# Square roots of the key norms on ScalarE for the first two chunk pairs, with a new instruction order

## The chip, the cores and the metric

The kernel runs on one core of a Trainium2 chip. The metric is the device time of one launch in microseconds. The five engines are TensorE (PE; its weight loads are shown as PEld), VectorE (DVE), ScalarE (ACT), GpSimd (POOL) and SyncE (SP), which here issues every DMA. The instructions of each engine stand in the trace in the order of the program.

## The reference

A delta-rule attention, written as a loop over 768 steps for 4 batches and 8 heads of 48 features, and behind it a feed-forward network (FFN) on its output, with 3072 tokens, 384 features and 2048 hidden units:

```python
k_n = k / (np.linalg.norm(k, axis=-1, keepdims=True) + 1e-06)
for t in range(S):
    y[:, :, t] = np.einsum('bhd,bhde->bhe', q[:, :, t], state)
    v_old = np.einsum('bhde,bhd->bhe', state, kt)
    state = state + bt[:, :, :, None] * np.einsum('bhd,bhe->bhde', kt, vt - v_old)

h = x @ w_in                       # x: y, tokens by features
sp = np.maximum(h, 0.0) + np.log1p(np.exp(-np.abs(h)))
out = (h * erf(sp)) @ w_out
```

## The kernel before

The 768 steps are cut into 12 chunks of 64, two chunks making a pair. The loop inside a chunk becomes linear algebra: a Gram matrix of the keys (`gram_mm` with the name "pg"), scaled by `gn` = -beta / norm² (`gram_d` for chunks 0 and 1, `gram_a` for the others), then the inverse of a triangular matrix, then a short chain per batch (`chain_u`, `chain_s`, `chain_y`, 48 chain steps j in all) that carries the state from chunk to chunk. The inverse of pair 0 is worked out on VectorE (`first_blocks`, 15 times `first_row`, `first_back`) and finished on TensorE (`first_w`, `first_x`); that of every other pair by 31 `solve_row` on GpSimd, with a way through DRAM before and behind it. `merge_t` to `merge_m2` put the halves together. Four chain steps make an FFN group of 256 tokens, 12 groups g in all: `x_max` to `x_lo` scale and split the input into two halves of 16 bits, `ffn1` (16 blocks for each group, numbered n through all groups) makes h, `e_sp` (softplus), `e_erf`, `e_mul`, `e_split` and `e_rest` make the activation of a unit of two blocks, and `ffn2` multiplies by w_out. The weights come as 64-bit numbers, twelve blocks of 512 KB for each matrix, and are turned into two 16-bit halves on the way: `w_load`, `w_low` (a shift on VectorE), `w_mask` (ScalarE), `w_bits` (merges the two on VectorE), `w_sum`, then `w_hi` and `w_lo`.

**The key norms.** For each pair sg, `norm_sq` (L183) squares k on ScalarE and `norm_sum` (L191) sums over the 48 features on VectorE, chunk by chunk. Then `norm_ops(sg, 0)` to `norm_ops(sg, 5)` issue eighteen VectorE instructions on a 128x32 tile, three at a time (L202 to L215): the maximum with 1e-30, an integer first guess of the inverse root, three Newton rounds of three instructions, norm, + 1e-6, reciprocal, and from it gn and ga. norm itself (nm) scales v in `put_v`.

**Tables.** `table` (L125 to L128) loads a ScalarE table set when the set asked for isn't the one loaded last: set 2 for erf, Abs in `w_sum`, and `clear_first`; set 24 for softplus. The Prelu of `w_mask` isn't in set 24, so where it falls between two softplus calls the compiler adds two loads more (in the trace at 101.88 and 105.43 us).

**The order.** Every step is entered as an event with a due time (`on`), the events are sorted, and `ORDER`, a tuple of 2523 indices, then gives the order in which they are issued. It sets the order on all five engines and nothing else does. The events `fill` are products of zeros on TensorE: 150 of them, 128x384 in 16 bits, stand between real steps up to the first FFN block. Three PSUM banks are shared by the Gram and chain steps, and two banks by the `ffn1` results, each freed by an `e_sp` and an `h_out`.

**The beginning, in this order.** SyncE loads the transposed keys of chunk 1, k of chunks 1 and 0, the transposed keys of chunks 0 and 3, beta of pair 0, a block of v, then w_in blocks and q. ScalarE does the two Squares first. VectorE does the two sums, all six `norm_ops(0, i)`, seven `gram_d`, `first_blocks`, the rows with some weight steps between them, `first_back(0)` (L329, the other triangle's copy `xd`) and `first_back(1)` (L327, `td`). `first_w` on TensorE reads only `td`. `first_copy` on ScalarE and `first_x` read `xd`.

Of the kernel before, what the change touches and what calls it, by code (L numbers as in the profile page):

```python
# [11 lines left out]
AF = mybir.ActivationFunctionType  # L12
ALU = mybir.AluOpType
# [42 lines left out]
XR = 3  # L56
YR = 6
S2A = (0, 1, 2, 3)
CP = (0, 1, 2, 3)
CM = (0, 1, 2, 3)  # L60
FB = 6.5
T0 = 55.0
SW = 4.6
C1, C2 = 2.0, 14.0


EG = {("pg", 1, 1): 2, ("pq", 0, 0): 0, ("pq", 0, 1): 1}
SET_ERF, SET_SP = 2, 24
HSC = 2.0 ** -23


@with_exitstack
def delta_ffn_kernel(ctx, tc, kT, qT, ktok, vtok, btok, w_in, w_out, cst, out):
    nc = tc.nc
    te, ve, se, ge, sp = nc.tensor, nc.vector, nc.scalar, nc.gpsimd, nc.sync

    con = ctx.enter_context(tc.tile_pool(name="con", bufs=1))
    io = ctx.enter_context(tc.tile_pool(name="io", bufs=2))
    at = ctx.enter_context(tc.tile_pool(name="at", bufs=1))
    sm = ctx.enter_context(tc.tile_pool(name="sm", bufs=3))  # L80
# [13 lines left out]
    def on(t, fn, *a, **kw):  # L94
        ev.append((t, len(ev), lambda: fn(*a, **kw)))

    def us(x):
        return (x - T0) / SW
# [24 lines left out]
    ts = [None]  # L123

    def table(i):  # L125
        if ts[0] != i:
            ts[0] = i
            se.add_instruction(mybir.InstLoadActFuncSet(name=nc.get_next_instruction_name(), act_func_set_id=i, ins=[], outs=[]))  # L128

    def clear_first():  # L130
        table(SET_ERF)
# [28 lines left out]
    st = [{} for _ in range(NC_)]  # L160
# [24 lines left out]
    nt = {}  # L185
# [7 lines left out]
    def norms(sg, w):  # L193

        w = slice(0, 2)
        names = ("ri", "t1", "nm", "ga", "gn")
        if sg not in nb:
            nb[sg] = [sm.tile([P, 2, BP], F32, tag=k, name=f"{k}{sg}") for k in names]
        n2, be = nt[sg][:, w], be_t[sg][:, w]
        ri, t1, nm, ga, gn = (x[:, w] for x in nb[sg])  # L200
        ii = ri.bitcast(I32)
        ops = [lambda: ve.tensor_scalar(n2, n2, 1e-30, None, op0=ALU.max),  # L202

               lambda: ve.tensor_scalar(ii, n2.bitcast(I32), 1, None, op0=ALU.logical_shift_right),
               lambda: ve.tensor_scalar(ii, ii, -1.0, float(0x5F3759DF), op0=ALU.mult, op1=ALU.add)]
        for _ in range(3):
            ops += [lambda: ve.tensor_tensor(t1, ri, ri, op=ALU.mult),
                    lambda: ve.scalar_tensor_tensor(t1, t1, -0.5, n2, op0=ALU.mult, op1=ALU.mult),
                    lambda: ve.scalar_tensor_tensor(ri, t1, 1.5, ri, op0=ALU.add, op1=ALU.mult)]
        ops += [lambda: ve.tensor_tensor(nm, n2, ri, op=ALU.mult),  # L210
                lambda: ve.tensor_scalar(nm, nm, 1e-6, None, op0=ALU.add),
                lambda: ve.reciprocal(ri, nm),
                lambda: ve.tensor_tensor(t1, be, ri, op=ALU.mult),
                lambda: ve.scalar_tensor_tensor(gn, t1, -1.0, ri, op0=ALU.mult, op1=ALU.mult),
                lambda: ve.tensor_scalar(ga, gn, -1.0, None, op0=ALU.mult)]  # L215
        for i in range(2):
            st[2 * sg + i].update((k, x[:, i, :]) for k, x in zip(names, nb[sg]))
        return ops

    no, nb = {}, {}  # L220

    def norm_ops(sg, i, w=0):
        if i == 0:
            no[sg, w] = norms(sg, w)
        for fn in no[sg, w][3 * i:3 * i + 3]:
            fn()
# [284 lines left out]
    def stage(nm, i, n=RW):  # L511

        return wb[nm].rearrange("p a b -> p (a b)")[:, DM + i * n:DM + i * n + n]
# [35 lines left out]
    def w_sum(nm, i):  # L549
        raw = wt[nm]["raw", i * WG + WG - 1]  # L550
        table(SET_ERF)
        n = WG * RW
        junk = raw.rearrange("p a b -> p (a b)").bitcast(BF16)[:, :n]
        se.activation(junk, stage(nm, i, n), AF.Abs, bias=0.0, scale=1.0, accum_out=wt[nm]["mx"][:, i:i + 1])
# [143 lines left out]
    def e_sp(g, u):  # L698
        G = fg[g]
        k, o = divmod(u * EU, NB)  # L700
        if ("L", k) not in G:
            G["L", k] = ff.tile([P, NB, GT], F32, tag="L", bufs=LB, name=f"L{g}_{k}")
        table(SET_SP)
        se.activation(unit("L", g, u), G["ph", u], AF.Softplus, bias=0.0, scale=G["ct"])  # L704
# [53 lines left out]
    def chain_at(j):  # L758
        if j < B:
            return us(38 + 2 * j)  # L760
        if j < 2 * B:
            return C1 + 0.6 * (j - B)
        if j < 3 * B:
            return C2 + 1.2 * (j - 2 * B)
        return j * NFF * SF / GS - NFF * SF - LEAD
# [8 lines left out]
    def gram(t, d, c, name):  # L774

        on(t - 1.5 * d, load_kf, c, "k" + name)
        for i in range(2):
            on(t + 0.9 * i * d, gram_mm, c, i, name)
            on(t + (0.35 + 0.9 * i) * d, gram_a if name == "pg" else gram_p, c, i)

    def norm_events(sg, t, d):
        for x in range(2):
            c = 2 * sg + x
            on(t - (2.4 - 0.6 * x) * d, load_step, c)
            on(t + 0.2 * x * d, norm_sq, c)
            on(t + (0.2 + 0.2 * x) * d, norm_sum, c)
            gram(t + (0.75 + 1.8 * x) * d, d, c, "pg")
            on(t + (2.05 + 1.8 * x) * d, to_dram, c)
        on(t - 2.3 * d, load_beta, sg)
        for i in range(6):  # L790
            on(t + (0.45 + 0.1 * i) * d, norm_ops, sg, i)

    on(-100, clear_first)
    on(-99, clear_second)
    on(-98, warm, WARM)
    for i in range(WU):
        on(us(2 + 0.28 * i), fill)
    for i, (fn, *a) in enumerate(((load_step, 0), (load_kf, 0, "kpg"), (load_step, 1), (load_beta, 0), (load_kf, 1, "kpg"), (load_cst,))):
        on(us(0.1 + 0.05 * i), fn, *a)
    on(us(1), first_init)  # L800
    on(us(8), w_neg)
    for i, t in enumerate(xm[0] + xm[1] + zz):
        on(us(3 + i), clear_x, t)
    on(us(0.5), clear_q)
# [18 lines left out]
    for i in range(6):  # L823
        on(us(9 + 0.5 * i), norm_ops, 0, i)
# [6 lines left out]
    for sg in range(1, NSG):  # L831
        t0, t1 = solve_start[sg], solve_end[sg]
        norm_events(sg, *((t0 - 4.6, 0.85) if sg < 4 else (t0 - 5.8, 1.0)))
        on(t0 - 1.25, to_blocks, 2 * sg)
        on(t0 - 1.2, to_blocks, 2 * sg + 1)
        on(t0 - 0.8, solve_init, sg)
        for s0 in range(31):
            on(t0 + (t1 - t0) * s0 / 31, solve_row, sg, s0)
        on(t1 + 0.02, put_blocks, 2 * sg)
        on(t1 + 0.03, put_blocks, 2 * sg + 1)  # L840
    for c in range(NC_):
        m = merge_at(c)
        if c > 1:
            d = 1.0
# [23 lines left out]
    for j in range(B * NC_):  # L868
        t = chain_at(j)
        d = 1.0 if j >= 2 * B else 2.6 / SW / CS  # L870
# [12 lines left out]
    for i in range(NRW):  # L883
        tb = 10 + 2.6 * i
        on(us(0.6 + 0.1 * i), w_load, "in", w_in.bitcast(I32), i, RI[i])
        on(us(tb), w_mask, "in", i)
        on(us(tb - 0.5), w_low, "in", i)
        on(us(tb + 1), w_bits, "in", i)
        if i % WG == WG - 1:
            on(us(tb + 2.8), w_sum, "in", i // WG)  # L890
    for i in range(NRW):
        t = WO + WD * i
        on(t - 0.9, w_load, "out", w_out.bitcast(I32), i, RO[i])
        on(t - 0.3, w_mask, "out", i)
        on(t - 0.35, w_low, "out", i)
        on(t + 0.1, w_bits, "out", i)
        if i % WG == WG - 1:
            on(t + 0.5, w_sum, "out", i // WG)
# [21 lines left out]
    for g in range(NG):  # L920
        x0 = chain_at(g * GS + GS - 1) + CS + 0.8 if g else chain_at(GS - 1) + 4.5 / SW
        d = 1.0 if g else 3 / SW
# [26 lines left out]
    ev.sort(key=lambda e: (e[0], e[1]))  # L949
    if ORDER:  # L950
        ev = [ev[i] for i in ORDER]
    E = mybir.EngineType
# [45 lines left out]
```

## Time and profile before

| | us |
|---|---|
| median of 3 runs (lowest, highest) | 665.86 (664.22, 668.76) |
| the profiled execution | 662.12 |
| its span, first to last instruction | 660.30 |
| TensorE busy | 626.5 (95%) |
| VectorE busy | 487.6 (74%) |
| ScalarE busy | 459.7 (70%) |
| of it 123 table loads by L128 | 157.8 |
| GpSimd busy | 367.8 (56%) |

| DMA, each | KB | us from issue to landing (median) |
|---|---|---|
| transposed keys, half a chunk (two for each chunk) | 192 | 3.6 |
| k of a chunk | 384 | 4.5 |
| a block of w_in | 512 | 8.4 |
| q, half a chunk | 192 | 3.6 |

The profile is of one execution. The shares are means over stages with different limits, so they are to be read by stretch. A matmul of 16-bit operands with 384 columns stands in the rows with its full latency; in a row of successive ones the step from one to the next is what counts. Tiles are named with buffer numbers left out, and early tiles share the memory of w_out: "w_out" in the rows of the first 40 us stands for the inverse of pair 0.

### The profile page before, as it was taken

To read this page: it belongs to the slowest core of one execution; us is meant where nothing else is said; L and a number is where in the kernel's file an instruction comes from. 1 tells how busy PE (TensorE), PEld (TensorE's weight loads), DVE (VectorE), ACT (ScalarE), POOL (GpSimd) and SP (SyncE) were. 2 spreads that over 40 slices of the span, in tenths; PEclk is the share of its full clock that TensorE was granted. 3 is DMA by queue.
4 is the path that set the end of the run, shared out by engine and by line. 5 is a ranking of instruction groups with operands and counts; after the bars stand their busy time and mean duration, and the time that the engine had idled before them with its cause. 6 is when DMAs were issued, how large, how long until landed. Compare 5 with 4: busy or idle time off the path is not lost.

```text
span 660.3 us, 22811 instructions
## 1 busy us (share of the span) xinstructions
PE 626.5 (95%) x9842; PEld 481.9 (73%) x9842; DVE 487.6 (74%) x1036; ACT 459.7 (70%) x684; POOL 367.8 (56%) x524
## 2 busy tenths in 40 slices
PE   6998997799999999999999999999998999999996
PEld 4656766577778787777877777777776777777764
DVE  4989979689878896888697679763958658486361
ACT  1558889979758874675766468958727677787852
POOL 5270489669996539995188971278972114222131
PEclk9769999979999999999999999999999999999999
DMA  9856761543042750145622133442024011000002
GB/s 236 329 179 196 183 197 50 119 90 63 3 100 69 166 106 12 34 124 124 141 57 69 37 72 71 104 103 46 2 59 86 17 32 26 1 14 16 12 11 48
DMA packets 76420, 56.19 MB, mean 85 GB/s; under 512 B 57184, under 2 KB 66528, under 8 KB 76320
## 3 DMA queue, kind: packets, MB, share of 16 engines
q1 hardware_dynamic: 76320, 54.74, 33.4%
q8 instruction: 77, 1.26, 0.8%
q14 instruction: 23, 0.19, 0.1%
HBM read 42.14 MB, written 12.58 MB: 83 GB/s over the span
## 4 chain that ended last, share of the span: by engine, by line
PE 45%; POOL 19%; DVE 14%; ACT 11%; DMA 5%; issue 5%; SPq 1%; POOLq 0%; DVEq 0%; ACTq 0%
PE ph L678 14%; POOL xb L364 7%; POOL tmp L363 7%; PE pr L739 6%; PE pr L740 5%; PE pr L741 5%; ACT L128 4%; POOL L L728 2%; PE warm L143 2%; PE pg L251 2%; POOL z L448 2%; DMA d<-A 2%; DVE H L713 2%; ACT L L709 2%; PE pc L488 2%
## 5 line engine op out<-in xcount | busy, mean ns | idle before, releaser
L678 PE MATMUL ph<-xh,w_in 128*128 128x256 f16 x1152 | 206.4, 273 | 7.7 <-ACT L L704 5.4
L678 PEld LDWEIGHTS <-w_in 128*128 128x128 f16 x1728 | 165.6, 98 | 36.0 <-issue 6.9
L728 POOL TENSOR_TENSOR L<-H,L 128x512 f16<-128x512 f32 x72 | 87.9, 1229 | 170.7 <-DVE L L724 79.6
L128 ACT ACT_TABLE_LOAD x123 | 157.8, 1283 | 2.1
L678 PE MATMUL ph<-xl,w_in 128*128 128x256 f16 x576 | 157.2, 273 | 0.3 <-DVE xl L666 0.3
L741 PE MATMUL pr<-w_out,L 128*128 128x384 f16 x384 | 125.6, 327 | 1.2 <-DVE L L728 1.2
L740 PE MATMUL pr<-w_out,L 128*128 128x384 f16 x384 | 125.5, 327 | 0.7 <-DVE w_out L615 0.7
L739 PE MATMUL pr<-w_out,L 128*128 128x384 f16 x384 | 125.7, 327 | 0.5 <-DVE L L724 0.5
L704 ACT ACTIVATE L<-ph,xct 128x512 f32<-128x512 f32 x96 | 65.3, 687 | 61.5 <-DVE H L691 50.5
L364 POOL TENSOR_TENSOR xb<-xb,tmp 128x31 f32<-128x31 f32 (+15 forms) x155 | 95.6, 617 | 12.2
L363 POOL TENSOR_TENSOR tmp<-gb,xb 128x31 f32<-128x31 f32 (+15 forms) x155 | 89.4, 576 | 23.2 <-DMA gb<-d 13.3
L448 POOL TENSOR_TENSOR z<-v,nm 64x192 f32<-64x192 f32 x96 | 58.9, 613 | 70.7 <-DMA v<-vtok 19.4
L713 DVE TENSOR_TENSOR H<-H,L 128x512 f32<-128x512 f32 x96 | 76.3, 803 | 28.5 <-ACT L L709 21.8
L691 DVE TENSOR_SCALAR H<-ph 128x512 f32<-128x512 f32 x72 | 49.1, 685 | 28.9 <-PE ph L678 21.1
L709 ACT ACTIVATE L<-L 128x512 f32<-128x512 f32 x96 | 58.0, 626 | 0.8
L741 PEld LDWEIGHTS <-L 128*128 128x128 f16 x384 | 37.6, 98 | 27.4 <-DVE L L728 1.6
L739 PEld LDWEIGHTS <-L 128*128 128x128 f16 x384 | 37.6, 98 | 22.7 <-DVE L L724 0.7
L740 PEld LDWEIGHTS <-L 128*128 128x128 f16 x384 | 37.6, 98 | 20.5 <-issue 0.2
L467 DVE TENSOR_TENSOR z<-pc,ga 64x192 f32<-64x192 f32 x80 | 28.4, 355 | 26.9 <-PE pc L461 23.5
L724 DVE CAST L<-H 128x512 f16<-128x512 f32 x72 | 45.3, 633 | 1.4
L661 ACT ACTIVATE xh<-pt,xsx 64x128 f16<-64x128 f32 (+1 forms) x72 | 25.9, 394 | 24.4 <-DVE xsx L528 17.5
L143 PE MATMUL warm<-zero 128*128 128x384 f16 x158 | 34.1, 366 | 2.2 <-issue 2.2
(160 smaller groups left out, 973.3 us busy)
## 6 DMA issues: line engine op xcount, KB each, us to landing
raw_in<-w_in SPq DMA_DIRECT2D x12, 512.0 KB, 8.4
raw_out<-w_out SPq DMA_DIRECT2D x12, 512.0 KB, 5.0
d<-A SPq DMA_DIRECT2D x20, 256.0 KB, 3.5
kpg<-kT SPq DMA_DIRECT2D x24, 192.0 KB, 3.6
k<-ktok SPq DMA_DIRECT2D x12, 384.0 KB, 4.5
v<-vtok SPq DMA_DIRECT2D x48, 96.0 KB, 2.5
qp<-qT SPq DMA_DIRECT2D x24, 192.0 KB, 3.6
out<-ob SPq DMA_DIRECT2D x48, 96.0 KB, 2.2
```

Of the source, the lines that this page charges most:

```text
L128: se.add_instruction(mybir.InstLoadActFuncSet(name=nc.get_next_instruction_name(), act_func_set_id=i, ins=[], outs=[]))
L363: ge.tensor_tensor(tv, G[:, s, s + 1:].unsqueeze(1).broadcast_to([P, ncol, nr]), Xv[:, :, s:s + 1].broadcast_to([P, ncol, nr]), op=ALU.mult)
L364: ge.tensor_tensor(Xv[:, :, s + 1:], Xv[:, :, s + 1:], tv, op=ALU.add)
L448: ge.tensor_tensor(zz[j % 6][h1, :, hb, :], vt[j][h1], st[c]["nm"][h1, cs].unsqueeze(2).broadcast_to([C, NP, D]), op=ALU.mult)
L678: te.matmul(ph, w[:, i, kt * P:kt * P + P], G[x][:, :, ksl], start=(m == 0), stop=(m == 8))
L704: se.activation(unit("L", g, u), G["ph", u], AF.Softplus, bias=0.0, scale=G["ct"])
L709: se.activation(Lu, Lu, AF.Erf, bias=0.0, scale=1.0)
L713: ve.tensor_tensor(Hu, Hu, unit("L", g, u), op=ALU.mult)
L728: (ge if (g * NFF // EU + u) % GLM else ve).tensor_tensor(G["gl", u], unit("H", g, u), G["gh", u], op=ALU.subtract)
L739: te.matmul(G["po"][a], gh[:, o, asl], wout_h[:, i, :], start=(i == 0), stop=False)
L740: te.matmul(G["po"][a], gh[:, o, asl], wout_l[:, i, :], start=False, stop=False)
L741: te.matmul(G["po"][a], gl[:, o, asl], wout_h[:, i, :], start=False, stop=(i == NFF - 1))
```

## The change

For pairs 0 and 1 the root comes from ScalarE: `norm_root` loads set 3, which holds Sqrt, and takes the root s of the clamped sum (128x32). One Newton round on VectorE follows, twice the norm = s + n2 / s, with the 1e-6 in the same instruction. `norm_ops(sg, 0)` is then the maximum alone, `(sg, 1)` and `(sg, 2)` three instructions each up to gn, and `(sg, 3)` two: ga, and the halving of nm. That is nine VectorE instructions and one on ScalarE for a pair. `w_sum` takes set 3 as well as set 2. `clear_first` asks for set 3.

```diff
-SET_ERF, SET_SP = 2, 24
+SET_ERF, SET_SQ, SET_SP = 2, 3, 24
+NSQ = 2
...
-    def table(i):
-        if ts[0] != i:
+    def table(i, *also):
+        if ts[0] != i and ts[0] not in also:
...
     def clear_first():
-        table(SET_ERF)
+        table(SET_SQ)
...
+        if sg < NSQ:
+            ops = [lambda: ve.tensor_scalar(n2, n2, 1e-30, None, op0=ALU.max), None, None,
+                   lambda: ve.reciprocal(ri, t1),
+                   lambda: ve.tensor_tensor(ri, n2, ri, op=ALU.mult),
+                   lambda: ve.scalar_tensor_tensor(nm, ri, 2e-6, t1, op0=ALU.add, op1=ALU.add),
+                   lambda: ve.reciprocal(ri, nm),
+                   lambda: ve.tensor_tensor(t1, be, ri, op=ALU.mult),
+                   lambda: ve.scalar_tensor_tensor(gn, t1, -4.0, ri, op0=ALU.mult, op1=ALU.mult),
+                   lambda: ve.tensor_scalar(ga, gn, -1.0, None, op0=ALU.mult),
+                   lambda: ve.tensor_scalar(nm, nm, 0.5, None, op0=ALU.mult)]
...
+    def norm_root(sg):
+        table(SET_SQ)
+        se.activation(nb[sg][1], nt[sg], AF.Sqrt, bias=0.0, scale=1.0)
...
     def w_sum(nm, i):
...
-        table(SET_ERF)
+        table(SET_ERF, SET_SQ)
```

The tuple `ORDER` is new throughout, 2521 indices now: four `norm_ops` calls are gone and two `norm_root` have come. Read back into events, it differs from the old one in places on every engine. Those spoken of later are these:

| engine | before | after |
|---|---|---|
| SyncE, beginning | keys 1, k 1, k 0, keys 0, keys 3, beta, v, w_in 4, q 0, q 1, w_in 7 | keys 1, k 0, keys 0, k 1, w_in 0, w_in 11, beta, q 0, w_in 4, w_in 6, q 1 |
| ScalarE, beginning | Square 0, Square 1, mask 9, mask 3, `gram_p(0, 0)` | Square 0, mask 0, Square 1, root 0, `gram_p(1, 1)`, mask 3 |
| VectorE, beginning | sum 0, sum 1, 18 norm operations, 7 `gram_d`, `first_blocks`, rows with 3 shifts and 2 merges, L329, L327 | shift 0, sum 0, sum 1, 7 norm operations, 6 `gram_d`, `first_blocks`, `gram_d`, rows with ga, the halving, 3 shifts and 1 merge, `gram_d`, L327, L329 |
| TensorE, before `first_w(1)` | 8 `warm`, Gram and pq products with 49 fills between and behind them | pq products (0, 0), (1, 0), (0, 1), (1, 1), then 46 fills |
| ScalarE, pair 1 | `first_x2`, `merge_e2`, load for `w_sum` | root 1, `first_x2`, two `merge_e2`, `w_sum` without a load |
| ScalarE, from the first softplus | sp 1, sp 0, masks, sp 2, erf 2, sums, sp 3, sp 6, `clear_first`, sp 4, erf 4, erf 0 | sp 1, mask, sp 0, sp 2, erf 2, sums, erf 0, sp 3, sp 6, sp 4, erf 4, erf 1, erf 3 |
| ScalarE, `clear_first` | event 596 | event 1708, between erf (5, 7) and sp (6, 5) |

"sp 1" stands for `e_sp(0, 1)`, "mask 0" for `w_mask("in", 0)`. By the same reading `table` issues 124 loads in place of 123; of them 9 instead of 11 fall between the first softplus and that of unit (1, 1).

## Rows read from the trace of the kernel before

**Rows 1.** Windows view: us and count by engine, TensorE clock, DMA share, GB/s

```profile
0.00:20.00 20.00, 13.52 (x330) 10.87 (x331) 11.27 (x34) 3.52 (x4) 9.60 (x18) 0.84 0.93 265
20.00:95.00 75.00, 69.02 (x1514) 47.44 (x1513) 64.59 (x148) 55.35 (x103) 35.84 (x52) 0.91 0.70 213
95.00:140.00 45.00, 35.54 (x509) 28.53 (x510) 38.58 (x88) 39.52 (x60) 32.22 (x47) 0.92 0.40 89
120.00:133.00 13.00, 8.88 (x111) 6.68 (x106) 8.53 (x14) 10.96 (x19) 8.30 (x11) 1.00 0.52 117
133.80:139.00 5.20, 5.20 (x69) 4.03 (x68) 5.08 (x11) 3.47 (x5) 0.79 (x2) 0.50 0.74 120
140.00:640.00 500.00, 493.21 (x7401) 386.11 (x7400) 369.73 (x762) 353.08 (x510) 285.88 (x405) 1.00 0.27 60
```

**Rows 2.** Chain of waits, start: start us, us, what

```profile
7.18 0.85 ACT w_out L183
...
8.05 1.82 DVE n L191 x2
...
9.90 0.39 DVE n L202
...
14.06 0.18 DVE ga L215
14.24 2.33 DVE w_out L264 x7
...
30.30 2.12 DVE w_out L329
32.43 1.83 DVE w_out L327
```

**Rows 3.** VectorE timeline: start us, us, line, operation, shapes, [idle before]

```profile
13.22 0.35 DVE L212 RECIPROCAL ri<-nm 128x32 f32<-128x32 f32 x1
...
23.33 0.42 DVE L543 TENSOR_SCALAR raw_in<-raw_in 128x512 int32<-128x512 int32 x1
23.86 0.69 DVE L547 SCALAR_TENSOR_TENSOR w_in<-w_in,raw_in 128x512 int32<-128x512 int32 x1
...
126.75 0.69 DVE L713 TENSOR_TENSOR H<-H,L 128x512 f32<-128x512 f32 x1 [3.74 <-ACT L L709]
```

**Rows 4.** SyncE timeline, first DMA issues: start us, us

```profile
0.74 0.87 SPq L232 DMA_DIRECT2D kpg<-kT  x2
...
4.46 0.42 SPq L171 DMA_DIRECT2D be<-btok  x1
```

**Rows 5.** The raw weight blocks' tile, 0 to 60 us: time to landing

```profile
DMA to landing us min/median/max: 4.0/8.4/9.8
```

**Rows 6.** The beta tile, 0 to 20 us: time to landing

```profile
DMA to landing us min/median/max: 6.3/6.3/6.3
```

**Rows 7.** ScalarE timeline: start us, us, line, operation

```profile
19.30 0.67 ACT L539 ACTIVATE w_in<-raw_in 128x512 f32<-128x512 f32 x1 [10.54 <-DMA raw_in<-w_in]
...
54.92 1.28 ACT L128 ACT_TABLE_LOAD   x1
...
117.03 1.28 ACT L128 ACT_TABLE_LOAD   x1
118.33 1.18 ACT L273 COPY qp<-pq 64x512 f32<-64x512 f32 x2
...
121.75 1.28 ACT L128 ACT_TABLE_LOAD   x1
```

**Rows 8.** TensorE timeline round the first inverse product: start us, us

```profile
25.70 6.35 PE L143 MATMUL warm<-zero 128*128 128x384 f16 x38
34.39 1.91 PE L340 MATMUL pw<-w_out 16*32 16x16 f32 x128 [2.33 <-DVE w_out L327]
36.23 3.06 PE L143 MATMUL warm<-zero 128*128 128x384 f16 x9
```

More of the change, by code (lines that the diff above doesn't have):

```diff
@@ L200, in norms @@
         ri, t1, nm, ga, gn = (x[:, w] for x in nb[sg])
+        if sg < NSQ:
[8 more added lines that the diff above has]
+                   lambda: ve.tensor_scalar(nm, nm, 0.5, None, op0=ALU.mult)]
+            for i in range(2):
+                st[2 * sg + i].update((k, x[:, i, :]) for k, x in zip(names, nb[sg]))
+            return ops
         ii = ri.bitcast(I32)
@@ L225, in norm_ops @@
         for fn in no[sg, w][3 * i:3 * i + 3]:
-            fn()
+            if fn:
+                fn()
+    def norm_root(sg):
+        table(SET_SQ)
+        se.activation(nb[sg][1], nt[sg], AF.Sqrt, bias=0.0, scale=1.0)
     def load_kf(c, name):
@@ L790, in norm_events @@
         for i in range(6):
+            if sg < NSQ and i > 3:
+                continue
             on(t + (0.45 + 0.1 * i) * d, norm_ops, sg, i)
+            if sg < NSQ and i == 0:
+                on(t + 0.5 * d, norm_root, sg)
     on(-100, clear_first)
@@ L823, in delta_ffn_kernel @@
     for i in range(6):
-        on(us(9 + 0.5 * i), norm_ops, 0, i)
+        if i < 4:
+            on(us(9 + 0.5 * i), norm_ops, 0, i)
+    on(us(9.2), norm_root, 0)
     on(us(14.5), first_blocks)
```

2 lines of the change are left out of this document (1 added, 1 removed).

## Prediction

> **What bounds the kernel now.** I read the busy time by stretch first. From 140 to 640 us TensorE is busy 493.2 of 500 us at full clock, so nothing that another engine saves there can shorten the run by more than the 6.8 us in which TensorE stands [rows 1]. What can move lies before. From 20 to 95 us TensorE looks busy, but part of that is filler (the `fill` products between dependent steps, which stay in the program in any order); VectorE is busy 64.6 of 75 us and is the engine nearest to its limit [rows 1]. From 95 to 140 us TensorE stands 45.0 - 35.5 = 9.5 us, and from 133.8 to 139 us it runs at a granted clock of 0.50, the lower of its two levels (1.2 instead of 2.4 GHz), after it had been busy only 8.9 of the 13 us from 120 to 133 [rows 1]. Those 5.2 us at half clock cost 2.6.
>
> Next the chain that ended last, at its beginning: Square, two sums, the maximum at 9.90, the norm instructions to 14.24 us, seven `gram_d`, and much later the two transposes L329 and L327 [rows 2]. All of that is on the path: TensorE stands 2.33 us until L327 is over, and then starts `first_w` at 34.39 us [rows 8]. Last, the ScalarE timeline: between 117 and 124 us it loads tables at 117.03 and again at 121.75 [rows 7], and VectorE waits 3.74 us, to 126.75, for an erf result that stands behind them [rows 3].
>
> **The norms of pair 0, taken alone.** Today gn is ready at 14.04 us, 4.14 us after the maximum began at 9.90 [rows 2]. The new chain from there: maximum 0.39 [rows 2], Sqrt, two reciprocals of 0.35 [rows 3], and four more VectorE operations on the same 128x32 tile. The sixteen of these in the old chain took (4.34 - 0.39 - 0.35) / 16 = 0.22 each with the step to the next, so a reciprocal is 0.37 with it. That is 0.39 + 0.74 + 0.88 = 2.0 plus the Sqrt. No Sqrt is in the trace. It can't well be under the 0.18 of a VectorE pass over as many elements, nor over the 0.85 of the Square over 768 columns [rows 2]; with 32 columns it is near the first, and I take 0.25. So 2.3 in place of 4.1 us: 1.9 us gained (1.3 to 1.9).
>
> **The wait put ahead of it.** The new order puts the mask of weight block 0 on ScalarE between the two Squares and its shift on VectorE ahead of both sums. Both wait for a 512 KB load, and everything for the norms is queued behind them. That load is the seventh DMA on SP's queue. The issues there follow each other at about 0.44 us (two took 0.87 [rows 4]), so it goes out at 0.74 + 6 x 0.44 = 3.4 us. When it lands is not in the trace; the loads of this tensor took 4.0 to 9.8 us [rows 5], which makes 7.4 to 13.2. The nearest row is the load of beta: it went out at 4.46 behind eight DMAs (six of 192 KB, two of 384, 1920 KB by the sizes in the profile's table) and took 6.3 us [rows 4, 6], so it landed at 10.8. The weight block ends 2048 KB of queue (four of 192, two of 384, its own 512), 128 KB more; at the 265 GB/s of the first 20 us [rows 1] that is 0.5 us, and I take 11.3. From there: mask 0.67 [rows 7], Square 0.85, sum 0.91, maximum 0.39 [rows 2], Sqrt 0.25, and 1.6 for the six operations: 16.0 us. The new table load (1.28 [rows 7]) runs on ScalarE after the Square, from 12.8 to 14.1, beside the sum and the maximum, and costs nothing; if the sum came out earlier it would be late by up to 1.28. So the Gram scaling starts at 16.0 and not at 14.24: 1.8 us later (2.7 earlier, when k is the later of the two, to 3.7 later). The root's gain is spent here.
>
> Row and skill differ on the table load. Here the load at 117.03 takes 1.28 us and the next copy begins at 118.33, with nothing between [rows 7]. The Trainium skill ("ScalarE: Activation LUTs", section "What ACT_TABLE_LOAD costs") gives every switch the same 1283 ns and another 1380 ns of drain. By that figure the root would stand on the path 1.4 us longer; the trace does not bear out the drain.
>
> **From the Gram scaling to the first product.** Today 14.24 to 34.25 us is 20.0 us on VectorE and ends with both transposes [rows 2]. `first_w` reads only the result of L327, and the new order runs that one first: 2.14 less. One `gram_d` more is ahead of it (2.33 / 7 = 0.33), and so are the two norm operations moved behind the fifth row (0.4); of the weight work there are three shifts and one merge, not three shifts and two merges, which is 0.7 less [rows 2, 3]. 20.0 - 2.1 + 0.3 + 0.4 - 0.7 = 17.9, so `first_w` can start at 33.9 + 0.1: 0.4 us earlier. Two terms can spoil it: the query load of chunk 1 is now queued behind three weight blocks, and its product stands ahead of 46 fills. At full clock the fills take 46 x 0.167 = 7.7 us, at half clock 46 x 0.34 = 15.6 (6.35 / 38 and 3.06 / 9 [rows 8]).
>
> **Pair 1 and the weights.** Nine operations instead of eighteen: 2 x 0.37 + 7 x 0.22 = 2.3 in place of 4.3 us, 2.0 off VectorE. It is busy 86% of that stretch [rows 1], not all of it, and pair 1 has gaps beside it; I count 1.4 (0 to 2.0). ScalarE loses the load at 54.92 (1.28 [rows 7]), since the weight sums accept the set of the root. Against it: `norm_root(1)` waits in ScalarE's queue for VectorE's maximum, with `first_x2` of chunk 1 and both `merge_e2` of chunk 0 behind it, and that maximum stands behind a weight merge that itself waits for ScalarE's mask of block 4. I set 0.5 for it (0 to 3). Up to the first FFN product: -0.4 - 1.4 + 0.5 = -1.3 us.
>
> **From 95 to 140 us.** `clear_first` stands in ScalarE's order between two softplus calls and there loads a table that the next softplus throws out: the pair at 117.03 and 121.75, 2.57 us [rows 7]. The new order puts it near event 1700, where it costs one load; ScalarE is busy 353 of 500 us there, so that is hidden [rows 1]. In addition the erf of unit (0, 0) now comes ahead of `e_sp(0, 3)`, so that its result lies ready when VectorE reaches `e_mul(0, 0)`. The 3.74 us for which VectorE waited there [rows 3] are gone; the 2.57 are inside them. What is late next is VectorE's own queue (38.6 of 45 us busy [rows 1]). If TensorE's first `ffn2` comes 3.7 us earlier, it stands about 5.7 us in this stretch, and I expect the clock to stay up: 2.6 more. Together -6.3 (0 to -12.1, all the standing and the half clock).
>
> **After 140 us** the order is shuffled on every engine, with the same work but three more table loads. I take the 6.8 us of standing as unchanged (half of it either way, 3.4).
>
> **Sum.** -1.3 - 6.3 = -7.6 on the profiled execution's 662.12 us (span 660.30 and 1.82 around it): 654.5. The median of the runs shown is 665.86, 3.74 higher; on that scale 658.3.
>
> **Rivals.** *A, the gain is swallowed.* The weight block lands at 13.2, not 11.3 (+1.9), or the fills run at half clock; and VectorE's queue, not the erf, sets the first `ffn2`, so that only the two loads are saved (-2.6). That gives -1.3 + 1.9 - 2.6 = -2.0, about 664 us, with -4 to +4 around it. For it speaks that VectorE is nearly full in both stretches; against it, that the 3.74 us wait is a plain wait for ScalarE. *B, slower: banks freed late.* After 140 us each `ffn1` needs a bank that a softplus must free. If the new order puts that softplus behind one more table load, TensorE stands the 1.28 us of the load [rows 7], and a stretch of standing can be followed by one like 133.8 to 139 us, 2.6 more [rows 1]: some 3.9 us for each such place. The second one uses up the gain, the fourth makes it 15.6 - 7.6 = +8.0, 674 us. Against it: only 6.8 us of standing in 500 today, and the counts of softplus, erf and FFN calls between the steps are alike. *C, more.* Standing and half clock in 95 to 140 go altogether (-12.1): with the start -13.4, 652 us.
>
> **Chances.** Forecast, -11 to -4: 0.55. A: 0.25. B: 0.13. C: 0.07. One per cent, 6.7 us, is about what a measurement of this kernel can tell from no change. Some 0.65 of the forecast lies beyond it, and all of C: faster 0.43; the rest of the forecast and A: same 0.44; B: slower 0.13. The forecast alone spans 655 to 662 us on the median's scale. The range 650.5 to 669.5 takes in A and most of C and leaves out B.
>
> **What would show it.** Right: L327 starts ahead of L329 and `first_w` at 33 to 35 us; no pair of table loads round `clear_first` before 140; TensorE standing under 6 us from 95 to 140 and no stretch at 0.5 behind it. Wrong: the second Square starting later than 13 us or earlier than 10; the fills before `first_w` taking 15 us; TensorE standing more than 12 us between 140 and 640. If `first_w` starts later than 36 us and the end is still earlier, the start was of no account and the whole gain is that of 95 to 140.

## The result and the profile after

The changed kernel takes 657.05 us (median of 4 runs, 656.84 to 662.17), the kernel before 665.81 in the same runs: ratio 0.9881, 95% interval 0.984 to 0.9921. On another chip the two took 659.27 and 666.67 us, ratio 0.9893 (0.9859 to 0.9927). So it is faster by 1.1 to 1.2%, 7.4 to 8.8 us, where 7.6 were forecast. The profiled execution took 656.84 us, its span is 654.8 us in place of 660.3.

The changed kernel's windows, to be laid beside [rows 1] (columns as there):

```profile
0.00:20.00 20.00, 13.62 (x337) 10.89 (x339) 9.36 (x24) 5.06 (x6) 9.13 (x16) 1.00 0.93 285
20.00:95.00 75.00, 68.05 (x1513) 46.94 (x1509) 61.87 (x140) 54.95 (x103) 38.71 (x55) 0.91 0.72 203
95.00:140.00 45.00, 39.88 (x683) 33.61 (x683) 40.76 (x93) 40.60 (x63) 34.60 (x50) 1.00 0.42 100
120.00:133.00 13.00, 11.98 (x169) 9.81 (x166) 11.53 (x27) 12.82 (x21) 5.93 (x10) 1.00 0.56 130
133.80:139.00 5.20, 5.16 (x151) 4.62 (x153) 5.12 (x5) 2.90 (x6) 4.61 (x4) 1.00 0.60 103
140.00:640.00 500.00, 491.70 (x7261) 382.65 (x7260) 361.57 (x762) 361.05 (x514) 276.93 (x403) 1.00 0.27 60
```

From 95 to 140 us TensorE stands 45.0 - 39.9 = 5.1 us in place of 9.5, and the half clock of 133.8 to 139 us is gone. From 140 to 640 it stands 8.3 in place of 6.8. VectorE has 2.7 us less to do from 20 to 95.

ScalarE's timeline of the changed kernel in the stretch of [rows 7] (start, us, line):

```profile
113.30 1.28 ACT L129 ACT_TABLE_LOAD   x1
114.59 0.69 ACT L723 ACTIVATE L<-ph,xct 128x512 f32<-128x512 f32 x1
...
120.60 0.68 ACT L723 ACTIVATE L<-ph,xct 128x512 f32<-128x512 f32 x1
121.30 1.28 ACT L129 ACT_TABLE_LOAD   x1
122.59 1.67 ACT L728 ACTIVATE L<-L 128x512 f32<-128x512 f32 x3
```

One load for the softplus (L723), one for the erf (L728), and none between the softplus calls: the pair round `clear_first` is away.

The beginning of the changed kernel's chain of waits, beside [rows 2]:

```profile
3.51 6.30 DMA raw_in<-w_in
...
9.84 0.69 ACT w_in L558
10.53 0.73 ACT w_out L184
11.28 1.28 ACT L129
12.57 0.24 ACT t L245
...
14.29 0.20 DVE gn L209
...
14.58 2.09 DVE w_out L283 x6
...
29.67 1.86 DVE w_out L346
31.52 0.14 issue
31.66 1.91 PE pw L359 x98
```

The chain begins with weight block 0, as forecast, but that lands at 9.82 us. L346 and L348 are the transposes L327 and L329 of before. `first_w` starts at 31.66 instead of 34.39 us, and yet the first FFN product starts at 94.91 us, before at 94.92. In these two executions, then, the start gave nothing and all 5.5 us of the span came later: 565.4 us from the first FFN product to the end before, 559.9 after.

### The profile page after: what moved, and what is told of

Same layout as the page of the kernel before. It is cut to its first block, busy times and chain, and to the rows that moved or that the text cites. A ratio compares the mean times of both kernels' runs of the same rounds, so it can differ in the third digit from the quotient of the medians.

```text
span 654.8 us, 22802 instructions
## 1 busy us (share of the span) xinstructions
PE 623.0 (95%) x9842; PEld 479.7 (73%) x9842; DVE 474.5 (72%) x1018; ACT 462.2 (71%) x687; POOL 361.6 (55%) x524
## 4 chain that ended last, share of the span: by engine, by line
PE 61%; ACT 11%; DVE 10%; DMA 6%; POOL 4%; issue 4%; SPq 3%; POOLq 0%; DVEq 0%; ACTq 0%
PE ph L697 19%; PE pr L758 8%; PE pr L760 7%; PE pr L759 7%; ACT L129 4%; PE pc L480 3%; PE pc L507 3%; PE warm L144 2%; PE pm L445 2%; ACT L L723 2%; PE pq L270 2%; PE pc L493 2%; PE pg L270 1%; POOL z L467 1%; DMA d<-A 1%
## 5 line engine op out<-in xcount | busy, mean ns | idle before, releaser
L747 POOL TENSOR_TENSOR L<-H,L 128x512 f16<-128x512 f32 x72 | 85.9, 1205 | 157.1 <-ACT L L741 72.4
L383 POOL TENSOR_TENSOR xb<-xb,tmp 128x31 f32<-128x31 f32 (+15 forms) x155 | 92.1, 594 | 12.2
L723 ACT ACTIVATE L<-ph,xct 128x512 f32<-128x512 f32 x96 | 65.3, 686 | 45.6 <-DVE H L710 37.3
L732 DVE TENSOR_TENSOR H<-H,L 128x512 f32<-128x512 f32 x96 | 72.2, 762 | 16.8 <-ACT L L728 16.3
L728 ACT ACTIVATE L<-L 128x512 f32<-128x512 f32 x96 | 58.6, 627 | 0.8
L743 DVE CAST L<-H 128x512 f16<-128x512 f32 x72 | 40.1, 563 | 1.4
```

The costliest lines, as they stand in the source:

```text
L383: ge.tensor_tensor(Xv[:, :, s + 1:], Xv[:, :, s + 1:], tv, op=ALU.add)
L728: se.activation(Lu, Lu, AF.Erf, bias=0.0, scale=1.0)
L732: ve.tensor_tensor(Hu, Hu, unit("L", g, u), op=ALU.mult)
L747: (ge if (g * NFF // EU + u) % GLM else ve).tensor_tensor(G["gl", u], unit("H", g, u), G["gh", u], op=ALU.subtract)
```

## The experiments

The runs below have different starts, so the table gives, from each profiled execution, the start of the first FFN product, the time from there to the end, and TensorE's standing in the first 45 us of that stretch with its mean granted clock. "Old order" is the kernel before with a part of the change, "new order" the changed kernel with a part undone. Ratio and interval are worked out from all runs, against the kernel before on the same chip; where the times spread, the ratio is not the quotient of the two medians. The last three columns come from one execution each, and not always a typical one: that of "old order, erf first" (660.97 us) is the fastest of its 12, that of "new order, more fills" (665.27) the slowest of its 12, and that of the last row (660.75) the slowest of its 6. The diffs show the events of the engine in question; "..." stands for events left out.

| run | median us | ratio (95%) | first FFN product | from there to the end | standing in 45 us, clock |
|---|---|---|---|---|---|
| before | 665.81 to 666.67 | 1 | 94.92 | 565.4 | 9.5, 0.93 |
| changed | 657.05 | 0.9881 (0.984 to 0.9921) | 94.91 | 559.9 | 5.1, 1.00 |
| changed again | 659.27 | 0.9893 (0.9859 to 0.9927) | 97.46 | 560.9 | 5.9, 1.00 |
| old order, loads out | 658.42 | 0.989 (0.9855 to 0.9925) | 97.16 | 558.9 | 5.1, 1.00 |
| old order, roots | 664.73 | 0.9969 (0.9944 to 0.9995) | 99.94 | 565.0 | 9.1, 0.96 |
| old order, both | 660.5 | 0.9909 (0.9876 to 0.9941) | 97.08 | 561.9 | 6.1, 0.96 |
| old order, erf first | 663.04 | 0.9984 (0.995 to 1.0019) | 95.39 | 563.8 | 9.4, 1.00 |
| old order, erf first, loads out | 661.12 | 0.9923 (0.9892 to 0.9954) | 98.17 | 561.2 | 4.7, 0.96 |
| new order, no roots | 663.22 | 0.9945 (0.9914 to 0.9976) | 101.72 | 558.8 | 5.2, 1.00 |
| new order, loads back | 663.23 | 0.9949 (0.9921 to 0.9977) | 99.54 | 562.2 | 6.2, 0.96 |
| new order, block later | 657.87 | 0.988 (0.9837 to 0.9923) | 94.33 | 559.1 | 5.9, 1.00 |
| new order, back order | 660.25 | 0.9915 (0.9879 to 0.9952) | 96.02 | 561.3 | 5.8, 1.00 |
| new order, more fills | 662.94 | 0.9933 (0.9904 to 0.9961) | 99.51 | 563.8 | 4.2, 0.96 |
| new order, block later, load out | 656.86 | 0.9871 (0.9834 to 0.9907) | 98.11 | 560.5 | 4.8, 0.96 |

**The two table loads alone.** The kernel before with one event moved:

```diff
 e_erf(0, 2)
+clear_first()
 ...
 e_sp(0, 3)
 ...
 e_sp(0, 6)
 ...
-clear_first()
 ...
 e_sp(0, 4)
```

> The kernel before, with one event moved: clear_first stands right behind the erf of unit (0, 2), where the erf table is in place, so that the two table loads between the softplus calls (117.03 and 121.75 us) are not issued. Theory L (the loads are the gain of 95 to 140 us): ScalarE is 2.6 us earlier at e_mul(0, 0), TensorE's standing in 95 to 140 us falls from 9.5 to 7 us or less, the clock stays at 1.00 behind it: 2.6 + 2.6 = 5 us less, about 661 us on the median of 665.8. Theory O (the order of erf and FFN calls is the gain): the wait of e_mul(0, 0) shrinks from 3.74 to about 1.2 us, but TensorE still stands 8 us or more and the half clock stays: 0 to 2 us less.

By the ratio (0.989, interval 0.9855 to 0.9925) this one move gives as much as the whole change (0.9881 and 0.9893). The windows of the first 45 us behind the first FFN product and of the rest, of the kernel before and of this one:

```profile
94.90:139.90 45.00, 35.54 (x512) 28.54 (x509) 38.57 (x89) 39.48 (x60) 32.32 (x47) 0.93 0.40 89
139.90:660.30 520.40, 508.54 (x7494) 395.14 (x7491) 373.29 (x768) 361.43 (x520) 290.10 (x408) 1.00 0.26 59
```

```profile
97.20:142.20 45.00, 39.89 (x681) 32.94 (x680) 41.35 (x95) 43.01 (x67) 36.16 (x52) 1.00 0.40 87
142.20:656.10 513.90, 500.79 (x7323) 388.87 (x7320) 364.69 (x761) 355.12 (x510) 282.55 (x403) 1.00 0.27 60
```

Standing falls from 9.5 to 5.1 us, the clock stays at 1.00, and the stretch to the end is 6.5 us shorter. Theory L, and more than its 5: 2.6 us of loads took 4.4 us of standing away.

**The erf first, loads left in.** The other half of the forecast's reason:

```diff
 e_erf(0, 2)
+e_erf(0, 0)
 ...
 e_sp(0, 3)
 ...
 e_erf(0, 4)
 ...
-e_erf(0, 0)
```

> The kernel before with one event moved: the erf of unit (0, 0) stands right behind that of (0, 2), ahead of the softplus of (0, 3) and of clear_first; the two table loads stay. Theory L (the loads themselves are the cost): the stretch from the first FFN product to the end stays at 564 us or more (565.4 in the kernel before), 665 to 667 us. Theory Q (what costs is that VectorE's e_mul(0, 0) waits for an erf queued behind two loads; any order that brings the erf ahead cures it): its wait of 3.74 us is gone, TensorE stands 6 us or less in the first 45 us of that stretch in place of 9.5, no half clock, 561 to 562.5 us, 661 to 663 us.

What VectorE waits for from 10 to 45 us behind the first FFN product (us in all, times, longest), first in the kernel before, then here:

```profile
DVE H L713 <- ACT L L709: 4.0, 2, 3.7
DVE A L258 <- PE pg L251: 0.6, 1, 0.6
DVE w_in L615 <- ACT w_in L590: 0.5, 1, 0.5
```

```profile
DVE w_in L615 <- ACT w_in L590: 4.1, 2, 3.1
DVE A L258 <- PE pg L251: 0.5, 1, 0.5
DVE H L713 <- ACT L L709: 0.2, 1, 0.2
```

The wait of 3.74 us [rows 3] is gone, and 3.1 of it is back one step on: the weight product (L590) is in the same ScalarE queue behind the same loads. TensorE stands 9.4 us as before, where Q forecast 6 or less: by the trace, theory Q falls. The time says less: the median, 663.04, is at the edge of Q's 661 to 663 us, but the interval of the ratio takes in no change. The half clock did not come this time, and with the same standing the stretch to the end is 1.6 us shorter (563.8 against 565.4); single traces scatter by more than that, so this is no measure of what the half clock costs.

**Both of them.** Loads out and erf first:

> The kernel before with both: clear_first where it loads nothing, and the erf of unit (0, 0) right behind that of (0, 2). Theory Q: one cure is enough, 558 to 560 us from the first FFN product to the end as with the loads out alone (558.9), 657 to 660 us. Theory A (they add): 556 us or less, 655 to 657 us.

561.2 us to the end and 661.12 us, where Q named 558 to 560 and 657 to 660, and A 556 or less and 655 to 657. It is no better than with the loads out alone: that they add is not borne out. TensorE stands 0.4 us less, and some half clock is back (0.96).

**Loads back in the new order.**

```diff
 e_sp(0, 3)
+clear_first()
 ...
 e_sp(0, 6)
 ...
-clear_first()
```

> The changed kernel with clear_first put back between the softplus calls of units (0, 3) and (0, 6), so that two table loads are issued there again. Theory L: 2.6 us more standing in 95 to 140 us and, if that brings the half clock back, 2.6 more behind it: 660 to 663 us. Theory O: ScalarE's queue has room there in the new order, TensorE stands at most 1 us more, the clock stays at 1.00: 657 to 658.5 us.

By the ratios, 0.9949 against 0.9893 and 0.9881, the two loads cost 3.7 to 4.5 us here, with intervals that only just meet (0.9921 to 0.9927). That is L's 2.6 to 5.2, and the time is just above its 660 to 663; O, with 657 to 658.5, falls. The trace alone would not decide it: it has 1.1 us more standing than the changed kernel and 562.2 us to the end against 559.9 and 560.9, but the same instructions behind the first FFN product take 559.1, 561.3 and 563.8 us in three of the runs below.

**The roots alone, in the old order.** `norm_root` behind the first group of norm operations of each pair, `ORDER` otherwise as before:

> The kernel before in its old order, with the roots of pairs 0 and 1 by ScalarE in place of three rounds. Theory S (the start sets the end): gn of pair 0 comes 1.9 us earlier than at 14.06, less if the table load is on the path, first_w at 32.5 instead of 34.39, and pair 1 gives 1 to 2 us of VectorE: the run is 2 to 4 us shorter. Theory W (waits further on take the start's gain back): first_w comes 1 to 2 us earlier, the first FFN product still starts at 94.5 to 95.5 us, and the run is within 1 us of the kernel before.

565.0 us to the end, as before, so nothing of the roots shows behind the first FFN product. VectorE's timeline of this run:

```profile
9.85 1.81 DVE L192 TENSOR_REDUCE n<-w_out 128x16 f32<-128x768 f32 x2 [8.79 <-ACT w_out L184]
11.70 0.18 DVE L203 TENSOR_SCALAR n<-n 128x32 f32<-128x32 f32 x1
...
13.63 0.19 DVE L209 SCALAR_TENSOR_TENSOR gn<-t,ri 128x32 f32<-128x32 f32 x1
```

From the maximum to gn it takes 2.12 us in place of 4.13: the root saves here what was forecast. But the two sums began at 9.85 us and not at 8.05 [rows 2], because k of the two chunks landed later in this execution, and so `first_w` starts at 33.64, only 0.75 us earlier. The median is 1.6 us lower (0.3 to 3.7 by the interval), between the two theories, and the interval reaches into both.

**The new order without roots.** The old three rounds, with `norm_root` left out: all groups of pair 0 together, and groups 2 to 5 of pair 1.

> The changed kernel in its new order, with the old three rounds for pairs 0 and 1 and no root. Theory W (the start's gain is taken back, the order is worth everything): gn of pair 0 comes 1.5 to 2 us later than 14.48, first_w at 33.5, first FFN product at 95 us as before, and the run keeps at least 6 of the 8.8 us of the change: 657 to 660 us. Theory S (the roots carry a part): first FFN product 2 us later or more, 660 to 663 us.

558.8 us to the end: the gain there needs no root. But the time is 663.22, not W's 657 to 660; it is at the edge of S's 660 to 663, and the first FFN product, at 101.72, is late, as S has it. The norm chain of pair 0 takes 3.93 us here, from its maximum at 12.99 to gn at 16.92, and 2.20 in the changed kernel (12.28 to 14.48). In the new order the roots are worth some 3.5 us (0.9945 against 0.9893 of 666, with intervals that just overlap), by this one trace all of it in the start, though the norm chain makes only 1.7 of it. Part of it may not be the root's own: the old rounds of pair 1 stand in one piece here, and ScalarE loads a table at 57.98 us for the weight sums.

**Both parts in the old order.** Roots, and `clear_first` behind `e_erf(0, 2)`:

> The kernel before in its old order with both parts and nothing else: clear_first behind the erf of unit (0, 2), so that no table load is issued for it, and the roots of pairs 0 and 1. Theory L+S (the two loads are the gain behind the first FFN product, the root that before it, the rest of the new order is worth nothing): 559 us from the first FFN product to the end, 7.3 less than the kernel before for the loads and 1 to 2 for the roots, 656 to 658.5 us, at or under the changed kernel. Theory O (the new order is needed): over the changed kernel by 2 us or more.

This kernel does not do what was meant. `clear_first` is the changed kernel's here and asks for set 3, and behind the erf set 2 is in place, so that it does load:

```profile
109.60 1.28 ACT L129 ACT_TABLE_LOAD   x1
110.89 0.63 ACT L728 ACTIVATE L<-L 128x512 f32<-128x512 f32 x1
111.54 1.28 ACT L129 ACT_TABLE_LOAD   x1
```

One of the two superfluous loads is still there, 1.28 us ahead of the weight sums. 660.5 us, not L+S's 656 to 658.5; the interval holds the changed kernel's ratio and that of the loads out alone. With the load in it the run decides neither theory: no gain from the rest of the new order is shown, and none from the roots on top of the loads, but neither is ruled out.

**The changed kernel again.**

> The changed kernel as it is, on one chip with the three kernels after it, because the profile of the kernel with the loads put back shows the first FFN product at 99.54 us where the changed kernel has it at 94.91, with the same instructions up to there. Theory N (the start of one program differs by up to 5 us from execution to execution, by landings and the granted clock; from the first FFN product on it doesn't): the times spread over 656 to 664 us, median 658 to 662, the stretch from the first FFN product to the end is again 559.9 us within 1. Theory F (a start of 95 us belongs to this program): 656.5 to 658 us, first FFN product at 95 us within 1.

Theory N, as far as the start goes. Its other half, that the rest does not differ, fails: behind the first FFN product the changed kernel, this run and the runs with the block later, the back order and more fills issue the same instructions, and from there to the end they take 559.9, 560.9, 559.1, 561.3 and 563.8 us. A difference of less than some 5 us between two single traces therefore shows nothing in that column. Up to the first FFN product the changed kernel, this run and the one with the loads back issue the same instructions, and reach it at 94.91, 97.46 and 99.54 us. Their windows of 30 to 45 and 45 to 66 us, in this order, and last those of the run with the block later (94.33):

```profile
30.00:45.00 15.00, 13.11 (x419) 8.30 (x420) 13.96 (x16) 11.35 (x20) 11.72 (x14) 0.66 0.62 196
45.00:66.00 21.00, 17.65 (x495) 12.86 (x495) 15.05 (x37) 14.73 (x25) 3.92 (x6) 0.92 0.60 179
```

```profile
30.00:45.00 15.00, 10.61 (x412) 6.73 (x412) 14.46 (x15) 10.85 (x20) 12.07 (x16) 0.84 0.67 210
45.00:66.00 21.00, 17.98 (x478) 12.10 (x478) 13.32 (x30) 12.85 (x22) 2.58 (x4) 0.79 0.55 172
```

```profile
30.00:45.00 15.00, 10.50 (x416) 6.64 (x414) 14.54 (x18) 10.41 (x18) 11.66 (x16) 0.82 0.70 220
45.00:66.00 21.00, 17.60 (x416) 12.12 (x414) 12.09 (x26) 11.76 (x22) 3.51 (x4) 0.72 0.50 145
```

```profile
30.00:45.00 15.00, 12.14 (x419) 7.64 (x420) 14.03 (x17) 11.38 (x20) 12.28 (x16) 0.66 0.63 199
45.00:66.00 21.00, 17.21 (x533) 12.92 (x534) 15.93 (x40) 15.50 (x27) 4.81 (x7) 1.00 0.61 188
```

The third number from the end is the granted clock. Where the half clock falls into 30 to 45 us (0.66), 45 to 66 is at or near full clock and the first FFN product comes at 94 to 95; where it falls behind 45 (0.79, 0.72), at 97.5 to 99.5. Over all fourteen traces the first product lies at 94.3 to 96.0 us where the clock of 45 to 66 is 0.95 or more, at 97.1 to 101.7 where it is under 0.9, and at 94.9 and 97.2 in the two with 0.92.

**Block 0 later.** The wait that the forecast charged 1.8 us for, taken away:

```diff
-w_mask('in', 0)
-w_low('in', 0)
 ...
 norm_root(0)
+w_mask('in', 0)
 norm_ops(0, 1)
 ...
 norm_ops(0, 2)
+w_low('in', 0)
```

> The changed kernel with the mask of weight block 0 moved behind the root of pair 0 and its shift behind the third group of norm operations: nothing of the norms waits for the 512 KB load any more. gn of pair 0 is ready at about 12.2 us in place of 14.48. Theory S (the start sets the end): first_w at 29.5 to 30.5 in place of 31.66, first FFN product and end 1 to 2 us earlier. Theory W (taken back before the first FFN product): end within 1 us of the changed kernel.

VectorE's timeline of this run:

```profile
13.17 0.19 DVE L208 TENSOR_TENSOR t<-be,ri 128x32 f32<-128x32 f32 x1 [0.53 <-DMA be<-btok]
...
13.84 0.42 DVE L283 TENSOR_TENSOR w_out<-pg,gn 128x256 f32<-128x256 f32 x1
...
21.99 0.43 DVE L562 TENSOR_SCALAR raw_in<-raw_in 128x512 int32<-128x512 int32 x1 [0.90 <-DMA raw_in<-w_in]
```

The Gram scaling starts 0.7 to 1.3 us earlier than in the two runs of the changed kernel (14.58, 15.17), not 2.3: now beta lands last. In the other run with the block later, the last one here, VectorE waits 1.40 us for beta, to 14.15, and the Gram scaling starts at 14.82, as in the changed kernel. At 21.99 the shift of weight block 3 waits for its own landing, and `first_w` starts at 31.58, as before the move (31.66, 31.88). The median is 1.4 us lower with intervals on top of each other. Theory W, as far as this can tell.

**The transposes in the old order.**

```diff
+first_back(0)
 first_back(1)
 ...
-first_back(0)
```

> The changed kernel with the two last transposes of the inverse in the old order, so that first_w waits for both. first_w starts 1.9 us later, at about 33.6. Theory S: first FFN product and end 1.9 us later. Theory W: end within 0.7 us of the changed kernel.

`first_w` starts at 34.40, 2.5 us later than in the run beside it; the first FFN product is at 96.02 and the median 1.0 us higher, inside the intervals. ScalarE's first copies of the other transpose's result, in the changed kernel and here:

```profile
33.41 1.24 ACT L352 COPY xm<-w_out 32x512 f32<-32x512 f32 x2 [5.66 <-DVE w_out L348]
```

```profile
32.53 1.25 ACT L352 COPY xm<-w_out 32x512 f32<-32x512 f32 x2 [2.13 <-DVE w_out L348]
```

Whichever transpose comes second has its own consumer waiting: `first_w` on TensorE for L346, these copies on ScalarE for L348.

**More fills.** Ten more filling products ahead of `first_w`:

> The changed kernel with ten more filling products ahead of first_w, 1.67 us at full clock, in the 2.2 us for which TensorE stands there. Theory K (standing there brings the half clock of 32 to 42 us, and that sets the start): the granted clock stays at 1.00 from 31 to 42 us, the first FFN product and the end come 2 to 4 us earlier, 655 to 657 us. Theory C (the copies on ScalarE behind the transpose that now comes second set the start, not TensorE): the clock rises, but first_x starts at 41 to 42 us as before, and the end is within 1 us of the changed kernel.

TensorE's and VectorE's timelines of this run:

```profile
25.44 9.27 PE L144 MATMUL warm<-zero 128*128 128x384 f16 x56
34.65 1.26 PE L359 MATMUL pw<-w_out 16*32 16x16 f32 x128
```

```profile
30.82 1.95 DVE L346 STREAM_TRANSPOSE w_out<-w_out 128x1024 f32<-128x1024 f32 x1
```

Neither theory, and no gain: the ratio is 0.9933 against 0.9893 and 0.9881, with intervals that overlap. The fills began at 25.44 instead of 21.81, since the query products ahead of them waited for landings (1.56 us at 20.38) and ran partly at half clock; so they were still running when L346 ended, and put `first_w` off to 34.65. The clock is 1.00 from 30 to 45 us, and 0.53 from 45 to 54: the half clock was moved, not avoided.

**Block later, and the load out.** `clear_first` right behind `norm_root(1)`:

> The changed kernel with the mask and shift of weight block 0 behind the norms, as in the run before, and clear_first right behind the root of pair 1, where it loads nothing: one table load less, behind 140 us. If that load is hidden, as forecast: the same as with the block later alone, 657.9 us, within 1. If a product waited for it: up to 1.3 us less, 656.6 us.

656.86 us, the lowest ratio of all, 0.9871 (0.9834 to 0.9907); not to be told from the changed kernel (0.9893) or from the run without the load moved (0.988). The load behind 140 us was hidden, as far as that can tell. No run is shown to beat the changed kernel.

## Why the prediction was right, and where its steps failed

**95 to 140 us (forecast -6.3): right in place and size, half wrong in its reason.** Standing 9.5 to 5.1 and the half clock away make 5.5 us from the first FFN product to the end (4.4, and 2.6 by the forecast's price of the half clock, less 1.5 of more standing behind 140). The forecast read -3.74 off the wait of `e_mul(0, 0)` and put the 2.57 us of loads and the erf's new place together as its cure. The runs separate them: the loads out alone give 6.5 us in the trace and a ratio of 0.989, the erf ahead alone leaves 9.4 us of standing and a ratio of 0.9984, not told from no change. The wait of one VectorE instruction was not the quantity to take over; ScalarE was the engine in arrears, without a pause from 111 to 131 us, and whatever was next in VectorE's queue waited for the same loads.

**The root (forecast 2.3 in place of 4.1 us): right.** Maximum to gn took 2.20 us, the Sqrt 0.23 (estimate 0.25). Its table load ended at 12.56, when the maximum had just ended at 12.46: 0.1 us of it was on the path. The Sqrt began 0.01 us after the load. The Trainium skill ("ScalarE: Activation LUTs", section "What ACT_TABLE_LOAD costs") adds 1380 ns of drain to each switch; this switch shows none.

**The wait for block 0 (forecast +1.8): too large.** The step that failed is "128 KB more; at the 265 GB/s of the first 20 us that is 0.5 us, and I take 11.3": it put the block's landing behind that of beta by the bytes of the queue. The block went out at 3.51, as forecast, and took 6.3 us, as long as beta had [rows 6] though it is far larger; it landed at 9.82 (its shift started at 10.1 to 10.5 in five more executions). The Gram scaling started at 14.58, and at 14.9 to 15.2 in four more, not at 16.0. And most of what the wait did cost is not to be had back: with the block later, beta and then block 3 take its place.

**Gram scaling to the first product (forecast 18.0): 17.1**, so `first_w` came at 31.66 in place of the forecast 34.0, outside the 33 to 35 us that the forecast named as its sign. But what follows was missing: the sum carried the start of `first_w` on to the first FFN product as if nothing else led there. In this pair of traces the lead of 2.7 us at `first_w` is 2.1 at the first `first_x` and gone at the second `merge_z`. TensorE before, then in the changed kernel:

```profile
44.04 1.24 PE L351 MATMUL pw<-w_out 32*16 32x16 f32 x128
...
66.07 1.20 PE L413 MATMUL pz<-xm,T 32*32 32x32 f32 x64
```

```profile
41.92 1.29 PE L370 MATMUL pw<-w_out 32*16 32x16 f32 x128
...
66.34 1.20 PE L432 MATMUL pz<-xm,T 32*32 32x32 f32 x64
```

"`first_w` reads only the result of L327, and the new order runs that one first: 2.14 less" left out that the result of L329 is read too, by ScalarE's copies. They begin behind it, at 33.41, and from there ScalarE has no pause; `first_w2`, which hands `first_x` its operand, was ready to start at 38.74 and ran at 40.59 in that queue. In the second trace of the changed kernel TensorE waited 1.10 us for it, until `first_x` at 41.24. From 45 to 66 us the clock is 0.92 here and 1.00 in the kernel before; how the lead goes there was not taken apart. Undoing this part of the order moved `first_w` by 2.5 us and the end by nothing that shows.

**Fills.** 46 in 7.65 us at full clock, as forecast (7.7). In the run with block and load moved they ran on the path, ending with `first_w` at 34.83 and no standing: the forecast's spoiler came in that execution.

**Pair 1.** The root waited 1.99 us in ScalarE's queue for the maximum, as the forecast feared (0.5, up to 3).

**The start in all (forecast -1.3).** The pair of traces says 0. That is one execution each, and the same instructions reach the first FFN product at 94.91 to 99.54 us. Part of that scatter is the landing of the first k: in the six traces of the old order the sums begin at 7.93 to 9.85 us, and the kernel before, at 8.05, had them early. By the medians on one chip, 7.4 us less, with 4.5 to 5.5 of it behind the first FFN product by single traces, the start is some 2 to 3 us better: a rough estimate, by difference. What part of this is the root and what the order stays open: in the old order the roots gave 1.6 us, in the new one about 3.5.

**The sum (forecast -7.6).** The pair of traces gives 0 for the start in place of -1.3, about -7.0 for 95 to 140 us in place of -6.3, and +1.5 behind it in place of 0: -5.5 in all. That the medians, -8.8 and -7.4, lie so close to the forecast is partly luck: terms missed in both directions, and the forecast was added up on an execution of 662.12 us, 3.7 under its median.

**After 140 us (forecast 0, up to 3.4 either way):** +1.5 us, inside. Nothing of the new order behind the first FFN product shows beyond the two loads: 558.8 to 563.8 us to the end without them, 558.9 and 561.2 in the old order with the loads out. Rival B's late banks did not come (8.3 us of standing, where 12 was its sign); rival A's swallowed start did, at another place than it named.

## What to carry to other kernels

Look in the queue of the busiest helper engine for an instruction that only sets a state, here a table load between two calls that need the other table: moving that one event was worth as much as the whole new order. When a wait is to be cured, ask what else stands behind the same instruction; if the next one in the waiter's queue does too, the wait only changes its name. Follow every reader of a result that is moved back, and where one program's start scatters by 5 us, compare from a common event on as well as from the span's start. Even then look at the medians of many runs: here the same instructions took 559.1 to 563.8 us from the common event on.

## What the hardware showed beyond that

The half clock of the start was not tied to a place in the program: the same instructions had it at 30 to 45 us (clock 0.66, then 0.92) in one execution and mostly at 45 to 66 us (0.82, then 0.72) in another. The first FFN product came 4.6 us later in the second. That the place of the half clock is the cause is a guess and not shown: a chain that is late for other reasons could as well have moved the half clock. In the one trace with more fillers ahead of `first_w` the half clock had moved and was not gone (1.00 from 30 to 45 us, 0.53 from 45 to 54).
